# Two products moved among the attention visits, k decays in halves, and w_out slices spread evenly

## The chip, the cores and the metric

One core of a Trainium2 chip runs the whole kernel. The metric is the device time of one execution in microseconds (us). Three runs of the kernel before took 639.23, 640.70 and 640.75 us; the median is 640.7. The profile is of one execution with a span of 638.3 us.

## The reference

A retention block (a linear attention with a decay for each head) is followed by a two-layer block with a SiLU between. Cut to what is computed:

```python
def _attn_ref(q, k, v):                      # q, k, v: (4, 8, 768, 64), float32
    B, H, S, D = q.shape
    gamma = 1.0 - 2.0 ** (-5.0 - np.arange(H, dtype=np.float32))
    scale = 1.0 / np.sqrt(D)
    state = np.zeros((B, H, D, D), dtype=np.float32)
    y = np.zeros_like(q)
    for t in range(S):
        state = gamma[None, :, None, None] * state + np.einsum('bhd,bhe->bhde', k[:, :, t], v[:, :, t])
        y[:, :, t] = scale * np.einsum('bhd,bhde->bhe', q[:, :, t], state)
    return y

def _moe_ref(x, w_in, w_out):                # w_in (512, 2048), w_out (2048, 512), float64
    h = x @ w_in
    g = h * (1.0 / (1.0 + np.exp(-h)))
    return (g @ w_out).astype(np.float32)

attn_out = _attn_ref(q, k, v)
x = attn_out.transpose(0, 2, 1, 3).reshape(B * S, H * D)      # (3072, 512)
result = _moe_ref(x, moe_w_in, moe_w_out)                     # (3072, 512), float32
```

The weights come as 64-bit floats, the rest as 32-bit floats.

## The kernel before

The recurrence is done in chunks of 128 steps: 6 chunks x 4 batches are 24 units, numbered n = 4 * chunk + batch. A *visit* m does the first part of unit m (transposes of k and q), the middle part of unit m - 1 (sums of k and v, scores, mask) and the last part of unit m - 2 (y, and the split of y into x). Four units make a *group* c of 512 tokens. A *product* (c, f) multiplies group c's x by slice f of w_in (128 columns). Each operand is split into a high and a low part, so a product is 12 matmuls: eight into ha, four into hb. Its result g = SiLU(h) goes to memory (gd) and is fetched again for the second layer, which begins after all 96 products.

A slice of w_in or w_out (64-bit floats) is turned into 32-bit floats by one ScalarE and six VectorE instructions, and a slice of w_in is then split by two of each:

```python
    def convert_w(i):

        if i + W_AHEAD not in staged:
            load_w(i + W_AHEAD)
        t = staged.pop(i)
        # ... (cut: tiles a, s, p; lo and hi words)
        with tc.issue_after(evac[0]) if evac else ExitStack():
            nc.scalar.activation(out=a.bitcast(FP32), in_=hi.bitcast(FP32), func=AF.Abs,
                                 scale=65536.0)
        # L195 to L204: five VectorE instructions, in order s = sign, a = clamped,
        # s = a << 3 | s, p = power of two of s, p = lo * 2^-52 * p
        # L210, later: w = s + p
    def take_w(after=None, parts=0):


        i = taken[0]
        taken[0] += 1
        if i >= 2 * NF:
            return
        with tc.issue_after(after) if after else ExitStack():
            rounded = convert_w(i)

        def finish():
            w32 = rounded()
            if i < NF:
                split = split_w(i, w32, "wi", scale, w_sb)
                if parts == 2:
                    next(split)
                    behind_mask.append(split)
                else:
                    list(split)
            else:
                nc.sync.dma_start(out=wo_dram[i - NF], in_=w32)

        if parts:
            behind_next.append(finish)
        else:
            with tc.issue_after(after) if after else ExitStack():
                finish()
    W_AHEAD = 2
    for n in range(EARLY):
        for name in "kqv":
            load(name, n)
        if n in (1, 4):
            load_w(n // 4)
```

The decays. k of a unit is multiplied by gk, in place, either by eight ScalarE instructions (one for each head) or by one on VectorE; q's factor gq moves on once in each chunk:

```python
    def next_chunk():
        for a in range(HP):
            nc.scalar.activation(out=gq[:, a, :], in_=gq[:, a, :], func=AF.Copy,
                                 scale=step[:, a : a + 1])
        # ...
    def scale_k(n):
        if 0 <= n < len(units):
            t = kqv["k"][n]
            if units[n][0] == NC - 1:
                t = t[:D]
            if n in (1, 3, 5, 7) or 2 * B <= n < 3 * B + 2:

                for h in range(H):
                    nc.scalar.activation(out=t[:, h, :], in_=t[:, h, :], func=AF.Copy,
                                         scale=gk[:, units[n][0], h : h + 1])
                return
            g = gk[: t.shape[0], units[n][0], :].unsqueeze(2).to_broadcast([t.shape[0], H, D])
            nc.vector.tensor_tensor(out=t, in0=t, in1=g, op=ALU.mult)

    def scale_q(n):
        c, b = units[n]
        t, g = (x if c > 0 else x[:, :, D:] for x in (qt[n], gq))
        nc.vector.tensor_tensor(out=t, in0=t, in1=g, op=ALU.mult)
```

The middle part's end and the visit:

```python
    def finish_a(n, sc, sums):

        c, b = units[n]
        am[n] = one.tile([128, 2, HP, D], FP32, tag="am", name=f"am_{n}")
        mask = nc.vector.tensor_tensor(out=am[n], in0=sc, in1=decay, op=ALU.mult).ins
        masked[:] = [mask]
        mid = one.tile([128, HP, D], FP32, tag="mid", name=f"mid_{n}", bufs=2)
        steps_of[n] = state.get(b), mid

        with tc.issue_after(mask):
            if c == 0:
                nc.scalar.copy(out=mid, in_=sums[:, 0])
            else:
                nc.vector.tensor_tensor(out=mid, in0=state[b], in1=sums[:, 0], op=ALU.add)
            if c < NC - 1:
                state[b] = one.tile([128, HP, D], FP32, tag="state", name=f"state_{n}",
                                    bufs=B + 2)
                nc.vector.tensor_tensor(out=state[b], in0=mid, in1=sums[:, 1], op=ALU.add)
# ...
    def visit(m):

        first, mid, last = (0 <= m - i < len(units) for i in range(3))
        if mid and m > 1 and units[m - 1][1] == 0:
            next_chunk()
        if first:
            stage_t(m)
        if last:
            scores, states_with, yp = stage_y(m - 2)
            scores()
        if mid:
            sc, sums = score_tile(m - 1)
            stage_s(m - 1, sums)
        if last:
            states_with(0)
        if mid:
            stage_a(m - 1, sc)
            with tc.issue_after(taken_out[0]) if taken_out else ExitStack():
                finish_a(m - 1, sc, sums)
            with tc.issue_after(masked[0]):
                while behind_mask:
                    list(behind_mask.pop(0))
            scale_q(m - 1)
        if m == 0:
            chunk_decays()
            first_chunk()
        if first:
            scale_k(m)
        if last:
            states_with(1)
            finish_y(m - 2, yp)
        for name, n in (("k", m + 2), ("q", m + 2), ("v", m + 1)):
            if n >= EARLY:
                load(name, n)
```

A product, and the storing of g (all but the last `keep` results that are pending):

```python
    pending = []

    def product_in(c, f):
        ha, hb = turn(f"ha_{c}_{f}"), turn(f"hb_{c}_{f}")
        for i in range(3):
            for kk in range(KIN):
                nc.tensor.matmul(hb if i == 2 else ha, lhsT=w_sb[f][:, i, ts(kk, 128)],
                                 rhs=xt[c][:, i, kk, :], start=kk == 0 and i != 1,
                                 stop=kk == KIN - 1 and i != 0)
        hs = hpool.tile([128, NT], FP32, tag="hs", name=f"g_{c}_{f}")
        copied[:] = [nc.scalar.activation(out=hs, in_=ha, func=AF.Copy, scale=ONE_E).ins]
        taken_out[:] = [nc.vector.tensor_tensor(out=hs, in0=hs, in1=hb, op=ALU.subtract).ins]
        with tc.issue_after(taken_out[0]):
            while behind_next:
                behind_next.pop(0)()
        nc.scalar.activation(out=hs, in_=hs, func=AF.Silu)
        pending.append((c, f, hs))

    def put_g(keep):
        while len(pending) > keep:
            c, f, g = pending.pop(0)
            nc.sync.dma_start(out=g_dram[c, f], in_=g)
```

hpool, from which hs comes, has three buffers; the raw y of groups 0 to 2 use the same three.

The schedule. The order on the TensorE is that of the program; the other engines' order is made by a scheduler from priorities and dependencies, and `issue_after` holds an instruction behind another.

```python
    for m in range(EARLY + 2):
        visit(m)
        if m in (3, EARLY):
            take_w(masked[0] if m == EARLY else None)

    half = NF // 2
    pairs = [(c, f) for f in range(4) for c in range(2)]
    three = [x for f in range(4, half) for x in ((0, f), (1, f), (2, f - 4))]
    rest = ([(2, f) for f in range(half - 4, half)] +
            [(c, f) for c in range(2) for f in range(half, NF - 4)])
    last = ([(c, f) for c in range(2) for f in range(NF - 4, NF)] +
            [(2, f) for f in range(half, NF)])
    groups = [(c, f) for c in range(3, NC) for f in range(NF)]
    steps = pairs + three + rest + last + groups
    takes = [(0, f) for f in range(half)]
    takes += [(2, half - 4), (2, half - 2)]
    takes += [(0, half), (0, half + 2), (1, half), (1, half + 2)]
    takes += [(0, NF - 4), (0, NF - 2), (2, half + 2), (2, half + 4)]
    takes += [(3, f) for f in (3, 7, 11, 15)] + [(4, f) for f in (3, 7, 11, 12, 14, 15)]
    takes += [(5, 0), (5, 3)]
    behind = {(1, f): lambda f=f: visit(EARLY + 2 + f) for f in range(4)}
    at = ([(1, NF - 1)] + [(2, f) for f in range(NF - 7, NF - 2, 2)] +
          [(c, 4 * i + 1) for c in range(3, NC - 1) for i in range(B)])
    for i, x in enumerate(at):
        behind[x] = lambda m=EARLY + 6 + i: visit(m)
    behind[0, NF - 2] = lambda: [late_y(b) for b in range(2)]
    behind[1, NF - 4] = lambda: [late_x(0), late_y(2), late_x(1), late_y(3)]
    behind[1, NF - 2] = lambda: late_x(2)
    behind[1, NF - 1] = lambda: [late_x(3), visit(EARLY + 6)]
    for n, (c, f) in enumerate(steps):
        product_in(c, f)
        if (c, f) in takes:
            take_w(taken_out[0], 2 if n < len(pairs) else int(n < len(pairs + three)))
        put_g(1)
        put_g(1)
        behind.get((c, f), lambda: None)()
        # ... (cut: in group 5 the slices of w_out are fetched and split, one a step)
```

Of the kernel before, what the change touches and what calls it, by code (L numbers as in the profile page):

```python
# [15 lines left out]
AF = mybir.ActivationFunctionType  # L16
# [15 lines left out]
def kernel(  # L32
# [27 lines left out]
    nc = tc.nc  # L60
    B, H, S, D = q.shape
# [11 lines left out]
    scale = 1.0 / math.sqrt(D)  # L73
# [53 lines left out]
    units = [(c, b) for c in range(NC) for b in range(B)]  # L127
    kqv = {"k": {}, "q": {}, "v": {}}
    EARLY = 2 * B
# [21 lines left out]
    staged = {}  # L151
# [20 lines left out]
    def convert_w(i):  # L172
# [6 lines left out]

        if i + W_AHEAD not in staged:
            load_w(i + W_AHEAD)
        t = staged.pop(i)
        if not wide:
# [6 lines left out]
# [3 lines that stand above are left out]
# [51 lines left out]
    W_AHEAD = 2  # L246
# [50 lines left out]
# [4 lines that stand above are left out]


    xt, kt, qt, am = {}, {}, {}, {}
    behind_next, behind_mask = [], []
    taken_out, copied, masked = [], [], []
    state, steps_of = {}, {}

# [22 lines left out]
    def scale_k(n):  # L330
        if 0 <= n < len(units):
            t = kqv["k"][n]
            if units[n][0] == NC - 1:
                t = t[:D]
            if n in (1, 3, 5, 7) or 2 * B <= n < 3 * B + 2:

                for h in range(H):
                    nc.scalar.activation(out=t[:, h, :], in_=t[:, h, :], func=AF.Copy,
                                         scale=gk[:, units[n][0], h : h + 1])
                return  # L340
            g = gk[: t.shape[0], units[n][0], :].unsqueeze(2).to_broadcast([t.shape[0], H, D])
            nc.vector.tensor_tensor(out=t, in0=t, in1=g, op=ALU.mult)
# [150 lines left out]
    def visit(m):  # L493

        first, mid, last = (0 <= m - i < len(units) for i in range(3))
        if mid and m > 1 and units[m - 1][1] == 0:
            next_chunk()
        if first:
            stage_t(m)
        if last:  # L500
# [6 lines left out]
            states_with(0)  # L507
        if mid:
            stage_a(m - 1, sc)
            with tc.issue_after(taken_out[0]) if taken_out else ExitStack():  # L510
                finish_a(m - 1, sc, sums)
            with tc.issue_after(masked[0]):
# [3 lines that stand above are left out]
# [15 lines left out]
    def product_in(c, f):  # L531
# [5 lines left out]
                                 stop=kk == KIN - 1 and i != 0)  # L537
        hs = hpool.tile([128, NT], FP32, tag="hs", name=f"g_{c}_{f}")
        copied[:] = [nc.scalar.activation(out=hs, in_=ha, func=AF.Copy, scale=ONE_E).ins]  # L539
        taken_out[:] = [nc.vector.tensor_tensor(out=hs, in0=hs, in1=hb, op=ALU.subtract).ins]  # L540
        with tc.issue_after(taken_out[0]):
            while behind_next:
# [54 lines left out]


    ctx.enter_context(tc.manual_schedule(engines={mybir.EngineType.PE}))
    for m in range(EARLY + 2):  # L600
        visit(m)
        if m in (3, EARLY):
            take_w(masked[0] if m == EARLY else None)

    half = NF // 2
    pairs = [(c, f) for f in range(4) for c in range(2)]
    three = [x for f in range(4, half) for x in ((0, f), (1, f), (2, f - 4))]
    rest = ([(2, f) for f in range(half - 4, half)] +
            [(c, f) for c in range(2) for f in range(half, NF - 4)])
# [1 line left out]
            [(2, f) for f in range(half, NF)])  # L611
    groups = [(c, f) for c in range(3, NC) for f in range(NF)]
    steps = pairs + three + rest + last + groups
    takes = [(0, f) for f in range(half)]
    takes += [(2, half - 4), (2, half - 2)]
    takes += [(0, half), (0, half + 2), (1, half), (1, half + 2)]
    takes += [(0, NF - 4), (0, NF - 2), (2, half + 2), (2, half + 4)]
    takes += [(3, f) for f in (3, 7, 11, 15)] + [(4, f) for f in (3, 7, 11, 12, 14, 15)]
    takes += [(5, 0), (5, 3)]
    behind = {(1, f): lambda f=f: visit(EARLY + 2 + f) for f in range(4)}  # L620
    at = ([(1, NF - 1)] + [(2, f) for f in range(NF - 7, NF - 2, 2)] +
          [(c, 4 * i + 1) for c in range(3, NC - 1) for i in range(B)])
# [99 lines left out]
```

## Time and profile before

| | |
|---|---|
| median of three runs | 640.7 us |
| span of the profiled execution | 638.3 us |
| ScalarE: scaling of k, kqv (units 1, 3, 5, 7) | 32 activations, 8.1 us |
| ScalarE: scaling of k, kf (units 8 to 13) | 48 activations, 12.9 us |
| VectorE: scaling of kqv (units 0, 2, 4, 6) | 4 instructions, 2.8 us |
| copy of ha by ScalarE | 96 x 592 ns |
| subtraction of hb by VectorE | 96 x 684 ns |
| DMA: a slice of w_out | 512 KB, 3.9 us to land |
| DMA: g stored, g fetched | 256 KB, 3.1 and 2.7 us |

How to read it: PE is the TensorE's matmuls, PEld its weight loads, DVE the VectorE, ACT the ScalarE, SP the engine that issues most transfers. A line number is that of the kernel before. A timeline line has the start and the length in us, the engine, the line, the operation, output <- input, the count, and in brackets the idle time before it with what ended that time. Matmuls overlap, so their lengths add up to more than the time they take; the distance between starts is what counts.

### The profile page before, as it was taken

How to read it: one execution, taken by the hardware profiler on the slowest of the kernel's cores; microseconds unless marked ns; L12 is line 12 of the kernel's file. 1: busy time of each engine (PE TensorE's matmuls, PEld its weight loads, DVE VectorE, ACT ScalarE, POOL GpSimd, SP SyncE). 2: the span in 40 equal slices, each digit the busy share in tenths (PEclk: the TensorE clock that was granted, in tenths of full speed). 3: DMA queues.
4: the chain of work that ended last, by engine and by line, in shares of the span. 5: the costliest groups of instructions: out<-in, count | busy, mean ns of one | idle time of the engine just before them, and what ended most of it. 6: DMA issues, size and time to landing. Idle time of an engine off the chain costs nothing. (4 is left out here: it accounts for less than half of the span.)

```text
span 638.3 us, 13569 instructions
## 1 busy us (share of the span) xinstructions
PE 611.7 (96%) x5440; PEld 505.8 (79%) x5440; DVE 419.9 (66%) x727; ACT 312.2 (49%) x622; POOL 6.7 (1%) x65
## 2 busy tenths in 40 slices
PE   5798989999999999999998999999999999999997
PEld 3686868888888888888887788888888888888785
DVE  1779888798978666666787797463544645554631
ACT  6698796666665545455465783231412221312311
POOL 2000000000000000000000000000000000000000
PEclk9989999999999999999999999999999999999999
DMA  9996877555677666555567674253432524342301
GB/s 200 208 212 150 232 203 225 172 159 189 200 207 199 192 183 190 183 177 175 205 218 251 202 226 130 85 167 97 135 129 79 186 68 132 131 129 83 120 0 67
DMA packets 123216, 103.66 MB, mean 162 GB/s; under 512 B 80016, under 2 KB 88464, under 8 KB 123152
## 3 DMA queue, kind: packets, MB, share of 16 engines
q1 hardware_dynamic: 120272, 97.54, 52.4%
q10 hardware_dynamic: 2880, 5.24, 2.2%
q8 instruction: 43, 0.70, 0.5%
q14 instruction: 21, 0.17, 0.1%
HBM read 66.06 MB, written 36.70 MB: 161 GB/s over the span
## 5 line engine op out<-in xcount | busy, mean ns | idle before, releaser
L535 PE MATMUL ha<-xt,wi 128*128 128x512 f32 x768 | 192.4, 392 | 1.9 <-issue 1.3
L535 PEld LDWEIGHTS ha<-xt,wi 128*128 128x128 f32 x768 | 142.7, 188 | 32.9 <-issue 1.5
L671 PE MATMUL o<-wo,gs 128*128 128x512 f32 x576 | 146.3, 389 | 0.0
L671 PEld LDWEIGHTS o<-wo,gs 128*128 128x128 f32 x576 | 108.1, 188 | 22.4
L589 DVE TENSOR_TENSOR gs<-gr,gs 128x512 fp32r<-128x512 f32 x96 | 62.3, 686 | 87.2 <-ACT gs L587 87.2
L671 PE MATMUL oa<-wo,gs 128*128 128x512 f32 x384 | 118.4, 389 | 0.1
L587 ACT ACTIVATE gs<-gr 128x512 fp32r<-128x512 f32 x96 | 53.6, 621 | 130.6 <-issue 129.9
L535 PE MATMUL hb<-xt,wi 128*128 128x512 f32 x384 | 103.5, 391 | 3.0 <-ACT g L539 2.9
L540 DVE TENSOR_TENSOR g<-g,hb 128x512 f32<-128x512 f32 x96 | 65.7, 684 | 42.2 <-ACT g L539 33.2
L535 PEld LDWEIGHTS hb<-xt,wi 128*128 128x128 f32 x384 | 71.5, 188 | 20.2 <-ACT g L539 5.3
L544 ACT ACTIVATE g<-g 128x512 f32<-128x512 f32 x96 | 60.5, 631 | 54.2 <-DVE g L540 54.1
L671 PEld LDWEIGHTS oa<-wo,gs 128*128 128x128 f32 x384 | 72.0, 188 | 15.4 <-DVE g L540 0.5
L671 PE MATMUL ob<-wo,gs 128*128 128x512 f32 x192 | 75.3, 392 | 0.3 <-DVE o L680 0.3
L539 ACT ACTIVATE g<-ha 128x512 f32<-128x512 f32 x96 | 56.8, 592 | 31.2 <-PE ha L535 24.9
L590 DVE SCALAR_TENSOR_TENSOR gs<-gs 128x512 fp32r<-128x512 f32 x96 | 62.2, 684 | 0.0
L671 PEld LDWEIGHTS ob<-wo,gs 128*128 128x128 f32 x192 | 36.0, 188 | 9.3 <-DVE o L680 2.0
L390 DVE TENSOR_TENSOR am<-sc,decay 128x512 f32<-128x512 f32 x24 | 16.5, 689 | 16.7 <-PE sc L382 16.7
L193 ACT ACTIVATE ca<-wf 128x512 f32<-128x512 f32 x32 | 21.5, 672 | 11.5 <-DMA wf<-in_moe_w_in_dram 3.3
L204 DVE SCALAR_TENSOR_TENSOR cp<-wf,cp 128x512 f32<-128x512 uint32 x32 | 22.1, 690 | 0.8
L200 DVE SCALAR_TENSOR_TENSOR cs<-ca,cs 128x512 uint32<-128x512 uint32 x32 | 22.1, 690 | 0.8
L679 ACT ACTIVATE o<-o 128x512 f32<-128x512 f32 x10 | 6.0, 600 | 33.1 <-PE o L671 32.7
L415 PE MATMUL y<-qt,mid 64*64 64x64 f32 x384 | 22.1, 231 | 0.0
(80 smaller groups left out, 548.3 us busy)
## 6 DMA issues: line engine op xcount, KB each, us to landing
gd<-g SPq DMA_DIRECT2D x96, 256.0 KB, 3.1
gr<-gd SPq DMA_DIRECT2D x96, 256.0 KB, 2.7
wf<-in_moe_w_out_dram SPq DMA_DIRECT2D x16, 512.0 KB, 3.9
out_dram<-o ACTq DMA_DIRECT2D x20, 256.0 KB, 2.1
wf<-in_moe_w_in_dram SPq DMA_DIRECT2D x16, 256.0 KB, 3.3
wf<-in_moe_w_in_dram SPq DMA_DIRECT2D x32, 128.0 KB, 3.8
kf<-in_k_dram SPq DMA_DIRECT2D x16, 256.0 KB, 5.0
qf<-in_q_dram SPq DMA_DIRECT2D x16, 256.0 KB, 4.3
```

The source lines that it names most:

```text
L193: nc.scalar.activation(out=a.bitcast(FP32), in_=hi.bitcast(FP32), func=AF.Abs, scale=65536.0)
L200: nc.vector.scalar_tensor_tensor(out=s, in0=a, scalar=3, in1=s, op0=ALU.logical_shift_left, op1=ALU.bitwise_or)
L204: nc.vector.scalar_tensor_tensor(out=p.bitcast(FP32), in0=lo, scalar=2.0 ** -52, in1=p.bitcast(FP32), op0=ALU.mult, op1=ALU.mult)
L415: i = nc.tensor.matmul(yp[ts(e, D), o, a, :], lhsT=lhsT, rhs=rhs, start=(e, o) not in started, stop=True, skip_group_check=True).ins
L535: nc.tensor.matmul(hb if i == 2 else ha, lhsT=w_sb[f][:, i, ts(kk, 128)], rhs=xt[c][:, i, kk, :], start=kk == 0 and i != 1, stop=kk == KIN ...
L539: copied[:] = [nc.scalar.activation(out=hs, in_=ha, func=AF.Copy, scale=ONE_E).ins]
L540: taken_out[:] = [nc.vector.tensor_tensor(out=hs, in0=hs, in1=hb, op=ALU.subtract).ins]
L544: nc.scalar.activation(out=hs, in_=hs, func=AF.Silu)
L587: nc.scalar.activation(out=t[:, 0, :], in_=g, func=AF.Copy, scale=HALF)
L589: nc.vector.tensor_tensor(out=t[:, 1, :], in0=g, in1=high, op=ALU.subtract)
L590: nc.vector.scalar_tensor_tensor(out=t[:, 2, :], in0=t[:, 1, :].bitcast(FP32), scalar=-1.0 / EPS, in1=high, op0=ALU.mult, op1=ALU.add)
L671: nc.tensor.matmul(o, lhsT=g, rhs=wo[f][:, i, :], start=first_ and i != 1, stop=last and i != 0)
```

## The change

It has four parts. Two products of group 0 are moved from the beginning of the joint stretch in among the last visits of groups 0 and 1: (0, 0) behind visit 6 and (0, 1) behind visit 8; slices 1 and 2 of w_in are converted earlier for it (behind visits 5 and 8) and slice 3 is loaded behind visit 7. The advance of gq is issued behind the scores and not ahead of the transposes' copies. The k of units 1, 3, 5 and 7 goes to VectorE, and for units 8 to 13 ScalarE scales four heads at once and the other four behind the copy of the next product. The twelve slices of w_out that were taken in groups 3, 4 and 5 are taken in groups 3 and 4 alone, six in each. All are meant to keep the TensorE from waiting for the other two engines.

```diff
--- before.py
+++ after.py
@@ -179,7 +179,7 @@
 
 
 
-        if i + W_AHEAD not in staged:
+        if i + W_AHEAD not in staged and i != 1:
             load_w(i + W_AHEAD)
         t = staged.pop(i)
         if not wide:
@@ -301,7 +301,7 @@
 
 
     xt, kt, qt, am = {}, {}, {}, {}
-    behind_next, behind_mask = [], []
+    behind_next, behind_mask, behind_copy = [], [], []
     taken_out, copied, masked = [], [], []
     state, steps_of = {}, {}
 
@@ -332,11 +332,15 @@
             t = kqv["k"][n]
             if units[n][0] == NC - 1:
                 t = t[:D]
-            if n in (1, 3, 5, 7) or 2 * B <= n < 3 * B + 2:
-
-                for h in range(H):
-                    nc.scalar.activation(out=t[:, h, :], in_=t[:, h, :], func=AF.Copy,
-                                         scale=gk[:, units[n][0], h : h + 1])
+            if 2 * B <= n < 3 * B + 2:
+
+                def half(heads):
+                    for h in heads:
+                        nc.scalar.activation(out=t[:, h, :], in_=t[:, h, :], func=AF.Copy,
+                                             scale=gk[:, units[n][0], h : h + 1])
+
+                half(range(H // 2))
+                behind_copy.append(lambda: half(range(H // 2, H)))
                 return
             g = gk[: t.shape[0], units[n][0], :].unsqueeze(2).to_broadcast([t.shape[0], H, D])
             nc.vector.tensor_tensor(out=t, in0=t, in1=g, op=ALU.mult)
@@ -493,8 +497,6 @@
     def visit(m):
 
         first, mid, last = (0 <= m - i < len(units) for i in range(3))
-        if mid and m > 1 and units[m - 1][1] == 0:
-            next_chunk()
         if first:
             stage_t(m)
         if last:
@@ -507,6 +509,8 @@
             states_with(0)
         if mid:
             stage_a(m - 1, sc)
+            if m > 1 and units[m - 1][1] == 0:
+                next_chunk()
             with tc.issue_after(taken_out[0]) if taken_out else ExitStack():
                 finish_a(m - 1, sc, sums)
             with tc.issue_after(masked[0]):
@@ -537,6 +541,9 @@
                                  stop=kk == KIN - 1 and i != 0)
         hs = hpool.tile([128, NT], FP32, tag="hs", name=f"g_{c}_{f}")
         copied[:] = [nc.scalar.activation(out=hs, in_=ha, func=AF.Copy, scale=ONE_E).ins]
+        with tc.issue_after(copied[0]):
+            while behind_copy:
+                behind_copy.pop(0)()
         taken_out[:] = [nc.vector.tensor_tensor(out=hs, in0=hs, in1=hb, op=ALU.subtract).ins]
         with tc.issue_after(taken_out[0]):
             while behind_next:
@@ -597,13 +604,23 @@
 
 
     ctx.enter_context(tc.manual_schedule(engines={mybir.EngineType.PE}))
+
     for m in range(EARLY + 2):
         visit(m)
-        if m in (3, EARLY):
-            take_w(masked[0] if m == EARLY else None)
+        if m == 3:
+            take_w()
+        elif m == 5:
+            take_w(masked[0])
+        elif m == EARLY - 2:
+            product_in(0, 0)
+        elif m == EARLY - 1:
+            load_w(3)
+        elif m == EARLY:
+            product_in(0, 1)
+            take_w(taken_out[0], 2)
 
     half = NF // 2
-    pairs = [(c, f) for f in range(4) for c in range(2)]
+    pairs = [(1, 0), (1, 1)] + [(c, f) for f in range(2, 4) for c in range(2)]
     three = [x for f in range(4, half) for x in ((0, f), (1, f), (2, f - 4))]
     rest = ([(2, f) for f in range(half - 4, half)] +
             [(c, f) for c in range(2) for f in range(half, NF - 4)])
@@ -611,12 +628,11 @@
             [(2, f) for f in range(half, NF)])
     groups = [(c, f) for c in range(3, NC) for f in range(NF)]
     steps = pairs + three + rest + last + groups
-    takes = [(0, f) for f in range(half)]
+    takes = [(1, 0)] + [(0, f) for f in range(2, half)]
     takes += [(2, half - 4), (2, half - 2)]
     takes += [(0, half), (0, half + 2), (1, half), (1, half + 2)]
     takes += [(0, NF - 4), (0, NF - 2), (2, half + 2), (2, half + 4)]
-    takes += [(3, f) for f in (3, 7, 11, 15)] + [(4, f) for f in (3, 7, 11, 12, 14, 15)]
-    takes += [(5, 0), (5, 3)]
+    takes += [(c, f) for c in (3, 4) for f in (0, 3, 6, 8, 11, 14)]
     behind = {(1, f): lambda f=f: visit(EARLY + 2 + f) for f in range(4)}
     at = ([(1, NF - 1)] + [(2, f) for f in range(NF - 7, NF - 2, 2)] +
           [(c, 4 * i + 1) for c in range(3, NC - 1) for i in range(B)])
```

## The prediction

> **What bounds the kernel now.** I read the page's busy shares first, then the busy time in windows of 20 us, then, in the windows that are not full, the timeline engine by engine.
>
> ```profile
> PE 611.7 (96%) x5440; PEld 505.8 (79%) x5440; DVE 419.9 (66%) x727; ACT 312.2 (49%) x622; POOL 6.7 (1%) x65
> ```
>
> The TensorE is busy for 611.7 of 638.3 us, so at most 26.6 us are there to be won, and not all of them: the windows (columns: stretch, its length, then busy us and instructions of each engine, granted clock, DMA share, GB/s) tell where they lie.
>
> ```profile
> 20.00:40.00 20.00, 15.66 (x525) 13.63 (x516) 16.81 (x32) 16.89 (x45) 0.36 (x4) 0.91 0.96 219
> 40.00:60.00 20.00, 16.49 (x478) 14.03 (x476) 18.35 (x36) 17.82 (x48) 0.27 (x3) 1.00 0.67 155
> 60.00:80.00 20.00, 18.87 (x396) 15.76 (x387) 17.20 (x33) 16.30 (x41) 0.27 (x3) 1.00 0.83 230
> 80.00:100.00 20.00, 17.43 (x203) 14.26 (x197) 17.98 (x34) 17.34 (x43) 0.09 (x1) 1.00 0.81 224
> 100.00:120.00 20.00, 20.00 (x90) 16.57 (x89) 16.23 (x28) 13.45 (x24) 0.00 (x0) 1.00 0.58 193
> 340.00:360.00 20.00, 18.40 (x80) 14.93 (x81) 15.79 (x27) 13.84 (x26) 0.00 (x0) 1.00 0.67 224
> ```
>
> From 100 us on the TensorE is full, but for 1.6 us at 340 to 360 and crumbs. Before 100 us nothing is full: from 20 to 100 us the TensorE stands idle for 4.34 + 3.51 + 1.13 + 2.57 = 11.5 us, while VectorE and ScalarE are each at 81 to 92%. That stretch is a chain passed among three engines. The first 20 us are bound by the loads (kqv and w) and lie before the change.
>
> ```profile
> 30.29 0.97 ACT L299 ACTIVATE gq<-gq,step 128x128 f32<-128x128 f32 x3
> 32.13 0.57 ACT L358 COPY kt<-kp 128x512 f32<-128x512 f32 x1
> 40.00 2.03 ACT L338 ACTIVATE kqv<-kqv,gk 128x64 f32<-128x64 f32 x8
> 339.29 0.66 ACT L193 ACTIVATE ca<-wf 128x512 f32<-128x512 f32 x1 [3.24 <-DMA wf<-in_moe_w_out_dram]
> ```
>
> ```profile
> 37.22 0.68 DVE L342 TENSOR_TENSOR kqv<-kqv,gk 128x512 f32<-128x512 f32 x1
> 50.13 0.69 DVE L200 SCALAR_TENSOR_TENSOR cs<-ca,cs 128x512 uint32<-128x512 uint32 x1
> 66.32 0.69 DVE L540 TENSOR_TENSOR g<-g,hb 128x512 f32<-128x512 f32 x1 [1.43 <-ACT g L539]
> 345.69 0.69 DVE L120 SCALAR_TENSOR_TENSOR wol<-wr,wo 128x512 f32<-128x512 f32 x1 [0.95 <-DMA wod<-cw]
> ```
>
> ```profile
> 50.91 0.73 PE L535 MATMUL ha<-xt,wi 128*128 128x512 f32 x2
> 52.94 1.55 PE L535 MATMUL ha<-xt,wi 128*128 128x512 f32 x6 [1.29 <-issue]
> 341.00 1.19 PE L535 MATMUL hb<-xt,wi 128*128 128x512 f32 x4 [1.06 <-ACT g L539]
> 348.24 2.11 PE L535 MATMUL ha<-xt,wi 128*128 128x512 f32 x8 [0.59 <-DVE g L540]
> ```
>
> To see: (1) at 30 to 32 us the advance of gq (L299) stands on ScalarE ahead of the copy of kt that the next scores wait for; (2) eight small activations that scale one k take 2.03 us of ScalarE, the same work on VectorE 0.68; (3) in the visits beside products VectorE waits 1.43 us for ScalarE to copy ha (later 0.82, 0.95, 0.81); (4) the first product starts only at 50.9 us; (5) at 339 us ScalarE waits for a slice of w_out from memory with a copy of ha behind it, and TensorE waits 1.06 and then 0.59 us.
>
> **What the Trainium skill says.** Its page "Perfetto Trace Analysis", section Optimization Strategy (under Identifying Performance Opportunities), says that a kernel with several regimes may gain by interleaving them. This is what the change does with two products; the windows above agree that visits leave the TensorE idle and products fill it. "TensorE: Matmul & The Clock Gate", section Architectural detail, says that ScalarE and VectorE work strictly first in, first out. The trace agrees: the wait of 3.24 us above held up an unrelated copy, so the order in a queue matters as much as its load. "ScalarE: Activation LUTs", What ACT_TABLE_LOAD costs: 186 ns + 0.833 ns per element, about 93 ns more for a scale read from memory, and 93 ns of overlap back to back. For 64 elements that is about 332 ns; the trace has 343 ns each and 2.03 us for eight.
>
> **The change part by part.** Units: a product is 12 matmuls in 2.72 us (from 335.25 to 337.97 us in the TensorE timeline where it is full). A visit costs a full TensorE about 3.2 us: 332 matmuls in the 20 us from 220 us are two visits of 136 and 60 of products; 60 x 0.227 = 13.6, and 6.4 remain for two. VectorE starts 128x512 operations 0.60 us apart, 128x256 ones and single-input scalar ones 0.33 apart, 0.45 where the next depends on it.
>
> *k of units 1, 3, 5, 7.* ScalarE loses 4 x 2.03 = 8.1 us, VectorE gains 4 x 0.60 = 2.4. Units 1 and 3 fall in the load-bound start; 5 and 7 matter.
>
> *gq behind stage_a.* Takes about 1.4 us of L299 out of the way of the kt copy, in the visit that starts at 27.8 us. The conversion of w_in slice 0 (between its mask and its state at 28.4 to 31.2 us before) now comes earlier in VectorE's order. I count 1.0 us: visit 6 cannot go before its k and q have arrived. The q of unit 5 came at 28.8 us (visit 5's transposes wait for it), that of unit 6 comes 0.79 MB later, which is 3.8 us at 205 GB/s: 32.6, and is transposed at 34.9 now, so at most 2.3 us are there.
>
> *Two products among visits, slice 1 converted at visit 5.* I take mask to mask (L390) as the measure of a visit. The masks before start at 33.88, 38.42, 41.88, 46.38, 51.92, 61.73, 71.92, 81.69, 91.50 for visits 5 to 13. For after I lay out VectorE's work in the order in which the built program has it, and take the larger of that and TensorE's work:
> - 5 to 6: mask, mid, q, state, two splits, k, and three conversion steps: 5.05 us (4.54 before);
> - 6 to 7: thirteen operations with five of the conversion, the g of product (0,0) and k: 7.0 (3.46); TensorE needs only 5.9;
> - 7 to 8: six operations, 3.06; the loop mask, state, next sums and scores rules, 4.0 (4.50);
> - 8 to 9: 6.1 with five steps of slice 2; TensorE 5.9: 6.1 (5.54);
> - 9 to 10: VectorE 4.6, TensorE 3.2 + 2.7 = 5.9: 5.9 (9.81);
> - 10 to 11: fourteen operations, 7.5 (10.19);
> - 11 to 12 and 12 to 13: two products, a visit, a whole conversion: 8.6 on VectorE, 8.6 on TensorE; 9.0 each (9.77 and 9.81), because the wait of 0.8 to 1.4 us for the copy of ha mostly goes: that is what the second half of k behind the copy is for, four activations or 1.0 us.
>
> The sum is 5.05 + 7.0 + 4.0 + 6.1 + 5.9 + 7.5 + 9.0 + 9.0 = 53.6 us against 57.6: 4.0 us won, with the 1.0 above 5.0. After visit 13 both kernels have the same work left.
>
> *w_out slices evenly.* Before, the slices at (4,14), (4,15), (5,0), (5,3) come one to three products apart and run into the splits of group 5. After, group 5 starts none, and takes are 2 to 3 products (5.4 to 8.2 us) apart, which is longer than the 3.9 us that a slice takes to land. The two waits, 1.06 + 0.59 = 1.65 us, should go; VectorE in groups 3 and 4 is at 65 to 81% and has the room. Won: 1.6.
>
> The sum of all is 6.6 us. I take off about 1.1 us for a wait I can't place (first rival): 5.5 us, so 640.7 - 5.5 = 635.2.
>
> **The rivals.**
> A: buffers of g. The results of (0,0) and (0,1) stay in two of the three buffers they share with the raw y until both are stored behind the product (1,0). In the new order the copies of y of unit 8 and of ha of (1,1) wait on those stores, which stand in the DMA queue behind loads of k and of w slice 4. Before, such waits were 1.42 and 1.4 us (for the stores of y and of g). For: only one buffer moves from visit 8 to visit 10. Against: the stores should be issued about 54 us and land in 3.1, before 60. It would cost 1 to 3 us: 636 to 638.
> B: VectorE becomes the bound. It is at 92% from 40 to 60 us, and the change gives it 2.4 us more. Then visits 6 to 9 take longer than my sums, by some 0.5 us each, and visits 10 to 13 win less: 637 to 638. For: three conversions' steps stand between mask and state. Against: the order shows them spread.
> C: more than counted. ScalarE's 8 us leave all latencies between VectorE and TensorE shorter; then visits 11 to 13 run at TensorE's 8.6 and visit 6 starts when its data arrive: 632 to 633.
> D: nothing from w_out, because other slices wait for their loads in groups 3 and 4: adds 1.6: 637.
>
> **Range and chances.** Sum without the deduction 634.1, the rivals 632 to 638: I predict 635.2 us, with 632.2 to 638.4 as the range. All idle TensorE time between 20 and 100 us and at 340 to 370 is 11.5 + 1.9 us; 2% is 12.8, so faster by more than 2% would take practically all of it: 0.02. Slower by more than 2% would need a serial wait of 13 us, of which the order shows no sign: 0.01. Within 2%: 0.97.
>
> **What would show it.** Masks of visits 5, 9 and 13 at about 32.9, 55 and 88.5 us (33.88, 51.92, 91.50 before); product (0,0) starting about 39 us; TensorE idle of 20 to 100 us down from 11.5 to about 6.5; no wait of VectorE over 0.8 us for the copy of ha in visits 11 to 13; TensorE full from 330 to 370 us; ScalarE's scaling of kqv gone. I am wrong if the mask of visit 13 is not at least 3 us earlier, if ScalarE waits over 1 us for a store of g, or if groups 3 and 4 show new TensorE waits.

## The result, and the profile after

The changed kernel took 639.8 us (median of four runs, 638.89 to 640.72) beside 640.0 us for the kernel before in the same session: ratio 0.9997, 95% interval 0.9974 to 1.002. The prediction was 635.2 us, with 632.2 to 638.4 as its range. The span of the profiled execution is 637.1 us (638.3 before).

The windows of the changed kernel, to be laid beside those of before (stretch, its length, busy us and instructions of TensorE, weight loads, VectorE, ScalarE, GpSimd, then granted clock, DMA share, GB/s):

```profile
20.00:40.00 20.00, 16.45 (x489) 14.29 (x488) 18.26 (x36) 13.36 (x28) 0.35 (x4) 0.91 0.93 217
40.00:60.00 20.00, 15.85 (x423) 13.22 (x421) 15.76 (x31) 14.34 (x35) 0.51 (x3) 0.83 0.66 144
60.00:80.00 20.00, 18.30 (x318) 15.46 (x319) 15.77 (x31) 15.96 (x41) 0.18 (x2) 0.91 0.76 203
80.00:100.00 20.00, 18.45 (x325) 15.67 (x324) 19.35 (x38) 17.59 (x44) 0.18 (x2) 1.00 0.83 231
340.00:360.00 20.00, 20.00 (x90) 16.55 (x89) 16.04 (x25) 17.63 (x34) 0.00 (x0) 1.00 0.69 203
```

The TensorE is now full at 340 to 360 us: the waits for slices of w_out are gone. From 20 to 100 us it still idles for 3.55 + 4.15 + 1.70 + 1.55 = 10.95 us, against 11.5 before. And there is something that no such window of before from 40 to 620 us had: the granted clock is 0.83 and 0.91 from 40 to 80 us. At half clock the eight matmuls of an ha start 0.45 us apart (51.81 to 55.39 below) and not 0.23 (335.25 to 337.06 before), while the TensorE counts as busy all the time, so its busy share hides part of the loss.

Where it is lost shows in the masks of visits 8, 9 and 10 on VectorE (start, length, engine, line, operation, output <- input, count):

```profile
49.83 0.69 DVE L394 TENSOR_TENSOR am<-sc,decay 128x512 f32<-128x512 f32 x1 [0.53 <-PE sc L386]
59.94 0.68 DVE L394 TENSOR_TENSOR am<-sc,decay 128x512 f32<-128x512 f32 x1
69.03 0.69 DVE L394 TENSOR_TENSOR am<-sc,decay 128x512 f32<-128x512 f32 x1 [1.00 <-PE sc L386]
```

All intervals from mask to mask, the predicted ones beside them:

| visits | 5-6 | 6-7 | 7-8 | 8-9 | 9-10 | 10-11 | 11-12 | 12-13 |
|---|---|---|---|---|---|---|---|---|
| predicted | 5.05 | 7.0 | 4.0 | 6.1 | 5.9 | 7.5 | 9.0 | 9.0 |
| measured | 5.51 | 7.01 | 3.80 | 10.11 | 9.09 | 7.36 | 8.65 | 8.67 |

Six of eight are within half a microsecond. The two that hold the products (0, 1) and (1, 0) took 7.2 us more than predicted, and mask 13 came at 93.71 us, 2.2 us later than before (91.50):

```profile
91.50 0.68 DVE L390 TENSOR_TENSOR am<-sc,decay 128x512 f32<-128x512 f32 x1
93.71 0.68 DVE L394 TENSOR_TENSOR am<-sc,decay 128x512 f32<-128x512 f32 x1
```

What the TensorE did in those two intervals, in its timeline:

```profile
46.86 0.69 PE L419 MATMUL y<-am,kqv 64*64 64x64 f32 x32 [2.06 <-ACT ys L454]
...
51.52 0.36 PE L419 MATMUL y<-qt,mid 64*64 64x64 f32 x1 [1.32 <-issue]
51.81 3.78 PE L539 MATMUL ha<-xt,wi 128*128 128x512 f32 x8
55.39 1.25 PE L539 MATMUL hb<-xt,wi 128*128 128x512 f32 x4
56.48 0.60 PE L360 MATMUL kp<-ident,kf 128*128 128x128 f32 x4
...
61.70 3.08 PE L539 MATMUL ha<-xt,wi 128*128 128x512 f32 x8 [1.85 <-ACT xt L466]
...
66.14 0.60 PE L360 MATMUL kp<-ident,kf 128*128 128x128 f32 x4
```

Product (0, 1) lasts from 51.81 to 56.48, 4.67 us, and (1, 0) from 61.70 to 66.14, 4.44 us. A product in the full TensorE takes 2.72 us. That is 1.95 + 1.72 = 3.67 us of the 7.2. Ahead of (1, 0) stands a wait of 1.85 us for its own x, and ahead of (0, 1) one of 1.32 us that no semaphore explains. Together 6.8 us. The windows of 5 us give the reason for the long products:

```profile
45.00:50.00 5.00, 2.66 (x127) 2.54 (x127) 4.44 (x9) 4.79 (x11) 0.09 (x1) 0.89 0.97 221
50.00:55.00 5.00, 3.67 (x16) 2.69 (x11) 3.17 (x6) 2.09 (x5) 0.00 (x0) 0.50 0.59 115
60.00:65.00 5.00, 3.30 (x10) 2.61 (x10) 3.18 (x7) 1.80 (x4) 0.00 (x0) 0.76 0.62 170
```

From 50 to 55 us, which is product (0, 1), the granted clock is 0.50. In windows of 0.5 us the half clock runs from 48.5 to 56.0 and from 62.5 to 66.0 us. So the theory was: the product (1, 0), now right behind visit 9, waits for an x that this visit makes, short idle stretches ahead of the products make the clock drop, and both together eat what the other parts bring. The rivals were: the parts bring nothing even alone; or the Silu of (0, 0), which stands ahead of the copy ys that the TensorE waits 2.06 us for, holds the chain up.

### The profile page after: what moved, and what is told of

Same layout as the page of the kernel before. It is cut to its first block, busy times and chain, and to the rows that moved or that the text cites. A ratio compares the mean times of both kernels' runs of the same rounds, so it can differ in the third digit from the quotient of the medians.

```text
span 637.1 us, 13560 instructions
## 1 busy us (share of the span) xinstructions
PE 613.2 (96%) x5440; PEld 509.1 (80%) x5440; DVE 421.7 (66%) x731; ACT 305.7 (48%) x590; POOL 7.5 (1%) x65
## 4 chain that ended last, share of the span: by engine, by line
PE 90%; SPq 3%; DVE 2%; ACT 1%; issue 1%; DMA 1%; DVEq 0%; ACTq 0%; POOLq 0%
PE ha L539 28%; PE o L687 20%; PE hb L539 13%; PE oa L687 13%; PE ob L687 7%; PE y L419 3%; SPq L145 3%; PE sc L386 1%; PE sc L376 1%; PE kp L360 1%; PE qp L360 1%; DMA kqv<-in_q_dram 1%; SPq L167 0%; DVE o L696 0%; SPq L165 0%
## 5 line engine op out<-in xcount | busy, mean ns | idle before, releaser
L539 PE MATMUL ha<-xt,wi 128*128 128x512 f32 x768 | 195.0, 396 | 1.9 <-ACT xt L466 1.9
L539 PEld LDWEIGHTS ha<-xt,wi 128*128 128x128 f32 x768 | 144.2, 190 | 32.9 <-ACT xt L466 2.0
L539 PEld LDWEIGHTS hb<-xt,wi 128*128 128x128 f32 x384 | 72.9, 190 | 15.5
L394 DVE TENSOR_TENSOR am<-sc,decay 128x512 f32<-128x512 f32 x24 | 16.5, 687 | 11.5 <-PE sc L386 11.5
```

## The experiments

Each was timed in five rounds beside the kernel before (12 to 22 runs of each kernel, 27 to 64 of the kernel before), except fetch_bare. Ratios are to the kernel before in the same session, and across rows only they can be compared. Single runs of one kernel lie up to 5 us below and 6 us above its median, so a span of one trace proves little: the trace of p01_late is of a run 2.2 us below its median, those of fill_10 and move_only are of runs 2.2 us above theirs.

| label | kernel | median, us | ratio | 95% interval |
|---|---|---|---|---|
| again | the change as it is | 639.6 | 0.9987 | 0.997 to 1.0004 |
| start_only | the change, w_out as before | 640.4 | 1.0001 | 0.9983 to 1.0019 |
| wout_only | before, w_out evenly | 638.8 | 0.9969 | 0.9952 to 0.9985 |
| k_gq_only | before, with k and gq (the k of unit 8 at once) | 638.1 | 0.9968 | 0.9954 to 0.9982 |
| no_move | before, with k, gq and w_out | 638.4 | 0.9959 | 0.9944 to 0.9975 |
| move_only | before, with the two products moved | 641.9 | 1.0018 | 1.0002 to 1.0035 |
| p01_late | (0, 1) behind visit 9 | 637.3 | 0.9947 | 0.993 to 0.9964 |
| fill | useless matmuls ahead of both waits | 637.7 | 0.9963 | 0.9947 to 0.9979 |
| fill_10 | only the second of them | 638.7 | 0.9955 | 0.9937 to 0.9972 |
| silu_late | the Silu of (0, 0) later | 638.7 | 0.9984 | 0.9967 to 1.0001 |
| p01_silu | p01_late and silu_late | 636.2 | 0.9949 | 0.993 to 0.9968 |
| w3_late | slice 3 of w_in loaded later | 639.3 | 0.9977 | 0.9962 to 0.9993 |

### The parts by themselves

again is the change repeated.

> The changed kernel itself, a second time. Theory (the start lost 2 us for good reasons): product (1,0) again waits 1.5 to 2 us for the x of unit 7, VectorE again waits over 2 us before the g of (0,1), and the granted clock again falls to about half somewhere between 45 and 68 us. Rival (chance: the profiled execution was an unlucky one): no drop of the clock there, and the mask of visit 13 two or more us earlier than the 93.7 us of the first trace. Time: 639 to 640.5 in both.

start_only keeps everything but the new list of takes, wout_only has nothing else:

```diff
-    takes += [(3, f) for f in (3, 7, 11, 15)] + [(4, f) for f in (3, 7, 11, 12, 14, 15)]
-    takes += [(5, 0), (5, 3)]
+    takes += [(c, f) for c in (3, 4) for f in (0, 3, 6, 8, 11, 14)]
```

> The changed kernel with the w_out slices taken as before; so the two products, the k and the gq alone. Theory: the start costs about 2 us, so 641.5 to 642.5, ratio 1.002 to 1.004, with product (0,4) beginning about 94 us against 91.8 before. Rival (start neutral, trace unlucky): ratio 0.998 to 1.001.

> The kernel before with nothing changed but the twelve slices of w_out taken evenly in groups 3 and 4. Theory: the gain of 2.8 us seen between 290 and 370 us belongs to this part alone, so about 637.2 us, ratio 0.9955. Rival (the gain needs the shifted start, or is given back in the second layer): within 1 us of before, ratio above 0.998.

k_gq_only is the kernel before with k of units 1, 3, 5 and 7 on VectorE, k in halves behind copies, and next_chunk() behind the scores. no_move adds the list of takes above.

> The kernel before with the k and gq parts alone (unit 8's k is scaled at once): products and w_out as before. Theory (these parts are good, the two products' places are what loses): 2 to 3 us faster than before, 637.5 to 638.5, the wait of VectorE for the copy of ha under 0.8 us. Rival (VectorE had no room for k): within 0.7 us of before.

> The kernel before with the k, gq and w_out parts, and the products and slices 0 to 2 of w_in where they were. If the parts add up (k and gq 0.9968, w_out 0.9969), the ratio is 0.9937, 4.0 us below before, and below the changed kernel by 3 us: then moving the two products is what spends the gain. If they overlap, 0.995 to 0.997.

move_only is the kernel before with the rest of the change, the two products and the conversions and loads that go with them (the list of pairs, the first list of takes and the load left out at slice 1 are also as in the change, not shown here):

```diff
-        if m in (3, EARLY):
-            take_w(masked[0] if m == EARLY else None)
+        if m == 3:
+            take_w()
+        elif m == 5:
+            take_w(masked[0])
+        elif m == EARLY - 2:
+            product_in(0, 0)
+        elif m == EARLY - 1:
+            load_w(3)
+        elif m == EARLY:
+            product_in(0, 1)
+            take_w(taken_out[0], 2)
```

> The kernel before with the products (0,0) and (0,1) moved among the visits and slice 1 converted early, and nothing else. By subtraction (0.9987 of the changed kernel against 0.9937 for the other parts together) it should be 1.005, about 3 us slower than before, with the half clock in (0,1) and (1,0) as in the changed kernel. Rival (the move loses only where VectorE has k as well): 1.000 or below, and no wait of 2 us ahead of visit 8's y.

w_out evenly brings 0.31%, 2.0 us, and k with gq brings 0.32%, 2.0 us; each interval excludes 1. Moving the products costs 0.18%, 1.2 us, alone; its interval excludes 1 only just, and 1.005 had been expected. In presence of the other parts it costs about as much: 0.9987 of the change against 0.9959 of no_move is 1.8 us, though these two intervals overlap. start_only, all of the start together, came out neutral at 1.0001 where a loss of 2 us had been expected: the gain of k and gq and the cost of the move about cancel. The rival that the parts bring nothing has fallen: the parts bring, and the move takes much of it back. Whether the gains of w_out and of k and gq add up (4.0 us) or overlap, as the 2.6 us of no_move would have it, stays open; the intervals allow both.

The trace of move_only has the wait ahead of (1, 0) too, 2.19 us, but (1, 0) ran there at a clock of 1.00; its half clock fell from 49.5 to 53.5 us, in visit 8. So the wait for x belongs to the order, and where the clock falls varies.

### The product that waits for its x

In the change (1, 0) comes right behind visit 9, which makes the last of its x. Its last y matmul ends at 59.85 us. ScalarE's timeline until the product starts at 61.70:

```profile
59.85 0.65 ACT L193 ACTIVATE ca<-wf 128x512 f32<-128x512 f32 x1
60.41 0.57 ACT L454 COPY ys<-y 128x512 f32<-128x512 f32 x1
61.02 0.63 ACT L466 ACTIVATE xt<-ys 128x512 fp32r<-128x512 f32 x1
```

The copy of y stands behind the first step of a slice's conversion, about 0.56 us; the copy and the rounding to x are the other 1.3 us. Before, (0, 0) stood between visit 9 and (1, 0), which started at 55.25 us with no wait. p01_late puts (0, 1) there (and scales the whole k of unit 8 at once):

```diff
         elif m == EARLY:
+            while behind_copy:
+                behind_copy.pop(0)()
+        elif m == EARLY + 1:
             product_in(0, 1)
             take_w(taken_out[0], 2)
```

> The changed kernel with product (0,1) behind visit 9 and not behind visit 8, ahead of (1,0) (the held-back half of unit 8's k is scaled at once). Theory (serial chain: (1,0) stands right behind the visit that makes its x): the wait of 1.85 us before (1,0) goes, and with it the drop of the clock in (1,0); 2 to 3.5 us are won, 636.5 to 638. Rival (VectorE is the bound from visit 6 on, so waits only change places): the mask of visit 13 stays at 93 us or later, within 0.7 us of the changed kernel.

```profile
54.70 2.11 PE L539 MATMUL ha<-xt,wi 128*128 128x512 f32 x8
...
57.55 1.98 PE L539 MATMUL ha<-xt,wi 128*128 128x512 f32 x8
...
60.27 0.60 PE L360 MATMUL kp<-ident,kf 128*128 128x128 f32 x4
```

This is its TensorE timeline: (1, 0) starts at 57.55 with no wait, since (0, 1) fills the time in which x is made. The two products take 5.57 us (54.70 to 60.27), the clock is 1.00 in every window of 5 us from 40 to 65 us, and from mask 8 to mask 10 it is 14.41 us instead of 19.20. Mask 13 comes at 89.32. By its ratio the time is 3.4 us below that of before; it is 2.3 us below that of the change (637.3 against 639.6, beside each other on one chip), and those two intervals don't overlap. It has the lowest ratio of this study, but the intervals of p01_silu, fill, fill_10 and also no_move overlap with its own. So the better place repairs the move; that moving products brings anything over no_move, which leaves them where they were, is not shown.

### The clock

fill leaves the order of the change and puts nine useless matmuls of 128x512 ahead of the transposes of visit 8 and eight ahead of (1, 0), both into banks that are overwritten next:

```diff
+            if n == EARLY and name == "kt":
+                filler(tp, 9)
...
+        if (c, f) == (1, 0):
+            filler(ha, 8)
```

> The changed kernel with 17 matmuls added that compute nothing of use: nine ahead of visit 8's transposes, into the bank those overwrite, and eight ahead of product (1,0), into its own ha, which it overwrites. They stand where TensorE waits 2.1 and 1.9 us anyway. Theory (the half clock is set off by these two waits and costs time by itself): (0,1) and (1,0) run at the full clock, 2.7 to 3.0 us each in place of 4.7 and 4.4, the waits stay as they are otherwise, and 2 to 3.5 us are won: 636.5 to 637.5. Rival (the waits cost, the clock is hidden behind VectorE and ScalarE): masks where they were, 639.3 to 640. If the clock falls although TensorE is kept busy, the idle time doesn't set it off.

> The changed kernel with the eight useless matmuls ahead of (1,0) alone. Theory (each wait sets off its own drop of the clock): (0,1) still takes 4.4 to 4.7 us at about half the clock, (1,0) 2.7 to 3.2, so half of the gain of the run with both, 0.5 to 1 us: ratio to before 0.997 to 0.9985. Rival (one long slow state from 48 us on): (1,0) stays at half clock for its first microseconds in spite of the filling.

The TensorE timeline of fill, and two windows:

```profile
51.71 0.21 PE L426 MATMUL y<-qt,mid 64*64 64x64 f32 x1 [2.18 <-issue]
...
52.03 2.11 PE L548 MATMUL ha<-xt,wi 128*128 128x512 f32 x8
...
54.89 0.60 PE L367 MATMUL kp<-ident,kf 128*128 128x128 f32 x4
...
60.19 2.12 PE L548 MATMUL ha<-xt,wi 128*128 128x512 f32 x8
```

```profile
50.00:55.00 5.00, 3.29 (x24) 2.67 (x24) 2.76 (x6) 2.83 (x8) 0.00 (x0) 1.00 0.76 179
60.00:65.00 5.00, 5.00 (x86) 4.09 (x88) 3.21 (x6) 2.80 (x9) 0.00 (x0) 1.00 0.54 148
```

With work that does nothing the clock stays at 1.00, (0, 1) takes 2.86 us (52.03 to 54.89) instead of 4.67 and (1, 0), from 60.19 to 63.05, 2.86 instead of 4.44. Mask 13 comes at 90.92 instead of 93.71. In fill_10, which lacks the first nine, the trace has (0, 1) slow again (3.04 us for its first eight matmuls) and (1, 0) at full speed: the two drops are separate.

In the times fill is 1.5 us better than the change by the ratios (0.9963 and 0.9987), and here the intervals overlap. fill_10 had been expected to bring half as much, 0.997 to 0.9985; it came out at 0.9955, no worse than fill. So no run shows that the drop at (0, 1) costs time. What separates the kernels is (1, 0): where the wait ahead of it is filled or (0, 1) stands there (fill, fill_10, p01_late, p01_silu) the ratios are 0.9947 to 0.9963 and the median granted clocks over the whole span 0.994 to 0.9965; where it is left as in the change (again, silu_late, w3_late) they are 0.9977 to 0.9987 and 0.992 to 0.9925. In the filled kernels x comes no earlier for it, so most of what p01_late recovers seems to be the clock's part, but this is argued: the intervals are too wide to share it out between the wait and the clock.

The traces show the mechanism; its worth in the median run is smaller than in the first trace. The granted clock over the whole span says why: it was 0.986 in that trace, 0.9925 in the median of 22 runs of the change, and 0.996 in those of before and of fill. Half clock for t us lowers it by t / 2 / 637, so against 0.996 the first trace has 12.7 us more at half clock and the median run 4.5, about a third (an estimate from these clocks). At half the speed 4.5 us cost at most some 2.2 us.

### The Silu ahead of the copy

> The changed kernel with the SiLU of (0,0), and the table load ahead of it, issued behind the copy and the split of unit 5's y and not ahead of them. Theory (first in, first out: the copy of y waits for a SiLU that waits for VectorE's subtraction): the 2.1 us wait of visit 8's first y matmul shrinks to about 0.7 to 1, 0.5 to 1.5 us won, and perhaps the clock of (0,1) with it; (1,0) still waits 1.9 us. 638 to 639. Rival (the gap is VectorE's 7 us between the masks of visits 6 and 7): mask of visit 7 and all behind it unchanged, 639.6.

> Both: product (0,1) behind visit 9, SiLU of (0,0) behind unit 5's y. If both waits cost, 636 to 637, below the 637.3 of p01_late alone; if the SiLU's place doesn't matter there, 637.3 again.

Issuing the Silu of (0, 0) behind visit 7's copies turned the wait of 2.06 us for ys into one of 2.1 us for the mask on VectorE, whose seven microseconds of visit 7 are what the TensorE waits for (6 to 7, as predicted). The masks did not move: 46.14, 50.18, 60.04 and 69.22 for visits 7 to 10 (46.03, 49.83, 59.94 and 69.03 in the change). That rival has fallen.

### The wait that no semaphore explains

The first clue is a count. The windows from 0 to the end of each such wait, of before, give the number of matmuls and of weight loads that had run:

```profile
0.00:44.58 44.58, 31.21 (x852) 26.30 (x853) 25.21 (x47) 32.75 (x96) 5.12 (x47) 0.92 1.03 208
0.00:48.84 48.84, 34.48 (x980) 29.20 (x981) 28.36 (x54) 37.01 (x109) 5.21 (x48) 0.93 1.01 207
0.00:52.94 52.94, 37.29 (x1107) 31.69 (x1108) 32.39 (x61) 41.08 (x122) 5.30 (x49) 0.94 0.98 201
```

They are 127 or 128 matmuls apart. In the change the wait ended at matmul 979, and in fill, which has nine more matmuls ahead, at 980, nine matmuls earlier in the visit:

```profile
0.00:51.71 51.71, 37.52 (x980) 31.53 (x980) 34.67 (x65) 31.10 (x73) 5.58 (x48) 0.97 1.00 205
```

So it belongs to a place in the stream of instructions, not to one instruction. 127 matmuls with their weight loads are 254 instructions, with a few others 256. The Trainium skill, "Runtime: NRT & Kernel Launch", section Instruction fetch mechanics, says that engines fetch instructions by DMA in blocks of 16 KiB, 256 instructions, mostly hidden. The profile of before agrees with the size: its instruction queue moved 43 packets and 0.70 MB, 16 KB each. And the number of packets follows that of the instructions: 43 for 10,880 matmuls and weight loads before, which are 42.5 times 256, and 47 for the 12,192 of fetch_bare below, 47.6 times 256.

w3_late tried to thin the data under way at that time:

```diff
-        elif m == EARLY - 1:
-            load_w(3)
         elif m == EARLY:
+            load_w(3)
             product_in(0, 1)
```

> The load of slice 3 of w_in (512 KB) is issued behind the loads of visit 8 and not behind those of visit 7, so that the DMA queue is 2 to 3 us shorter at 48 to 52 us. In the traces so far the TensorE's waits put down to "issue" end at matmul 220, 347, 480, 600, 727, 852, 980 or 1106 of the program, some 127 apart, whatever instruction stands there (with nine useless matmuls ahead of it, it was still the 980th). 127 matmuls with their weight loads are 254 instructions[...], and the instruction queue moves 43 packets of 16 KB. Theory: at these places the TensorE waits for its next instructions, which stand behind data in the DMA engines; then the wait at the 980th matmul (1.32, 1.48 and 2.03 us in three traces) goes below 0.8 us, product (0, 1) starts about 1 us earlier and the time is 0.5 to 1.5 us below that of the changed kernel, ratio 0.996 to 0.998. Rival: instructions come in blocks but their fetch doesn't depend on the data under way, or the wait is for something else that is tied to visit 8: then it stays at 1.3 us or more at the 980th matmul, and the ratio is that of the changed kernel, 0.9987.

The wait was 2.35 us, at matmul 980 again. The load went behind those of visit 8, which were issued in its place, and the DMA engines were as full as before (243 GB/s from 47 to 51.2 us, 219 in the change), so this run said nothing of the data. Its ratio, 0.9977, lies where the theory had it, but the wait did not shrink, so the theory does not explain it; the interval takes in the ratio of the change. fetch_bare measures the fetch by itself. It computes nothing of the reference: 3048 matmuls of 64x64 in a row, and 24 loads of 256 KB.

> The disputed wait by itself. The kernel leaves the whole computation out: 3048 matmuls of 64x64, in the form of the y products, stand one behind the other with no wait among them, and from the 1017th on 24 loads of 256 KB, in the form of those of k, q and v, run beside them. Theory (instructions are fetched in blocks of 127 matmuls with their weight loads, and the fetch stands behind data): in the first 1016 matmuls no gap, or gaps under 0.3 us; in the second 1016, under loads at 200 GB/s or more, gaps of 1 us or more at every 127th matmul or nearly so, and none elsewhere. Rival 1 (the fetch is slow by itself, whatever the data): the same gaps in the first 1016 as in the second. Rival 2 (the waits in the visits are for something of the visit): no gaps in either.

Nothing held the loads back, so they ran from the start to about 33 us, and what was meant for the second part was measured in the first. Each matmul of the program stands twice in the records. TensorE timeline, with loads beside it in the first two lines and without in the last two:

```profile
20.08 2.09 PE L45 MATMUL one<-t 64*64 64x64 f32 x128 [0.91 <-issue]
24.63 2.71 PE L45 MATMUL one<-t 64*64 64x64 f32 x128 [2.46 <-issue]
...
82.64 2.09 PE L45 MATMUL two<-t 64*64 64x64 f32 x128 [1.36 <-issue]
86.09 2.09 PE L45 MATMUL two<-t 64*64 64x64 f32 x128 [1.36 <-issue]
```

After 128 records (256 instructions) comes a gap, every time, with or without loads. The first rival, a supply that is slow by itself, is the main part: without loads a block comes every 3.45 or 3.73 us though it takes only 2.09 to execute. Loads add to it: beside them, at 199 GB/s between 10 and 33 us, the blocks are 4.0 to 4.55 us apart. The theory that data alone make the gap has fallen. At the very start 223 records ran before the first gap, so somewhat under two blocks had come by then.

This can bound visits. A visit has 136 matmuls, 136 / 127 of a block: an estimate from these rates is 3.7 us without and 4.3 to 4.9 us beside loads. The waits of before shown above are 4.26 and 4.10 us apart, beside 193 and 133 GB/s: where visits follow one another with no product between, the kernel before kept about the pace at which the bare stream gets its instructions. That this, and not the other two engines, set its pace there is argued from the match and not shown.

## Why the prediction was wrong

**The step that failed** is the line "8 to 9: 6.1 with five steps of slice 2; TensorE 5.9: 6.1" with the next, "9 to 10: VectorE 4.6, TensorE 3.2 + 2.7 = 5.9: 5.9". They took 10.11 and 9.09 us. In each an interval was taken as the larger of two engines' work, with a visit at 3.2 and a product at 2.7 us as in a full TensorE. The runs showed three things in its place:

- *The chain.* (1, 0) waits 1.85 us for the x that visit 9 makes: y, copy, rounding, product, one after the other, with 0.56 us of a conversion ahead of the copy. The path through ScalarE was missing from the sum. p01_late removes the wait, and the kernel gains 2.3 us on the change.
- *The clock.* 3.67 us in the trace, since the products ran at half clock for much of their time; fill removes it. The prediction took 2.7 us for each product, its time at full clock. In the times a gain shows only where something differs at (1, 0), and the clock's share of it can't be told from the chain's.
- *The instruction block.* 1.32 us ahead of (0, 1) in the change, 1.3 to 2.4 us in the other traces with the same order. The prediction shows the "issue" wait of 1.29 us in the lines of before and gives it no cost in these sums. Before had such waits too, and no run removed this one, so what it costs stays open.

The 1.1 us taken off were for the first rival, the buffers of g, and covered none of this. In the first trace the start was 7.2 us worse than predicted (5.0 won against 2.2 lost). Less the 1.1 taken off, and less the 1.2 that w_out brought above its 1.6 in this trace, that leaves 4.9; the medians differ from the prediction by 4.6. That these agree so well is in part luck, as single runs spread by more; by start_only's ratio the start is neutral, 5 us short of the prediction. And not all of it is explained: p01_late, which repairs the order, is 3.4 us below before and not 5.5. "After visit 13 both kernels have the same work left" held, from mask 13 to the product that starts at 335.25 (before) and 337.30 us (after) it is 243.75 and 243.59 us: it is the start that was not won.

**What was right.** w_out: 1.6 us predicted, 2.0 measured alone; in the traces the product that starts at 335.25 before starts at 337.30, and the second layer at 369.94 instead of 370.66 us, so 2.8 us are won between. k and gq: they bring 2.0 us alone. In the change, mask 5 came at 33.51 instead of the predicted 32.9 us. Rival B's site, visits 6 to 7 under VectorE, took its 7.0 us. Product (0, 0) started at 37.51 (about 39 predicted). From visit 11 on VectorE waits at most 0.46 us for the copy of ha. The busy time of ScalarE fell by 6.5 us and that of VectorE rose by 1.8.

**The rivals.** A, buffers of g: in the visits up to 105 us ScalarE has no wait for a store of g; the longest for a store there is 1.63 us, for y, up to 100.34 us. Later there is one of 1.91 us, up to 219.59 us, where before had one of 1.41; so this sign of being wrong came true too, but the TensorE is full there (5.00 of 5 us) and nothing hangs on it. B: interval 6 to 7 was as summed, and what came on top in 8 to 9 and 9 to 10 is named above and lies on the TensorE. C and D fell. The signs that I had named decided it: mask 13 was to be 3 us earlier and was 2.2 later, and the idle time was to be 6.5 us and was 10.95.

## What to carry to other kernels

When work is moved to fill an idle engine, look up which instruction makes its input and what then stands between the two: a sum of each engine's work is no interval. Idle stretches of about two microseconds ahead of heavy matmuls can cost twice, once as idle time and once by the clock after them, so put a product that is ready there before one that is not. And try a move against its own absence: here the repaired move could not be told from leaving it out. In the bare stream many small matmuls in a row were paid by the instruction: count them per microsecond. Spreading them among large ones should help; no run here tested that by itself.

## What the hardware showed that was not expected

**Half clock after short gaps.** The Trainium skill, "TensorE: Matmul & The Clock Gate", section What's actually happening, says that the clock goes to half after at least one idle window of about 3.4 us and comes back after a busy one. Here shorter gaps came ahead of it: in the change one of 2.06 us that ended at 46.86, with half clock from 48.5, and one of 1.85 us that ended at 61.70, with half clock from 62.5. fetch_bare has the two sides in two windows, the first with a gap of 2.19 us ahead of it, the second with gaps of 1.36 and 1.64 us in every 3.5:

```profile
15.50:20.00 4.50, 3.64 (x128) 3.47 (x128) 0.00 (x0) 0.00 (x0) 0.62 1.02 224
40.00:60.00 20.00, 12.37 (x768) 11.56 (x764) 0.00 (x0) 0.00 (x0) 1.00 0.02 5
```

A TensorE that idles 38% of its time in gaps of up to 1.64 us kept full clock from 33 to 176 us; gaps of 2.19 and 2.46 us were each followed by half clock, though these had loads beside them and the short ones had none. It is not a sharp rule: fill had an issue wait of 2.18 us and move_only a wait of 2.19 us ahead of (1, 0), and both kept 1.00, while in no_move the half clock came at 54.5 us, after gaps of only 1.52 and 1.55 us.

**Instructions as a bound.** The Trainium skill's section on instruction fetch, named above, calls the cost of a block's end mostly hidden. For 64x64 matmuls it was not: 256 instructions took 2.09 us to execute at full clock, and the next 256 started 3.45 to 4.55 us after them.
